# A tuned convolution and two feed-forward layers on one core: a new order of issue, the band in two halves, and other accumulators for block 1

## The chip, the cores and the metric

The program runs on one core of a Trainium2 chip. The core has a matmul engine (PE, with PEld its weight loads), a vector engine (DVE), an activation engine (ACT), a general engine (POOL) and a queue engine that issues most transfers (SP). Each works through its own list of instructions in order and waits on semaphores for the others. The metric is the device time of one execution in microseconds. The kernel before took a median of 1347.27 us over 3 runs (1347.11 to 1349.38).

## What is computed

Three stages follow each other on 8192 tokens (2 sequences of 4096) of 192 values. The first is a causal convolution of 7 taps, whose weights are a softmax per head; the two others are a product to 2048 hidden values, a function of each of them, and a product back to 192.

```python
out = np.einsum('hk,bskhg->bshg', softmax(weight), x_unf)       # 8 heads of 24 values
h = x @ w_in;   g = h * clip(h + 3, 0, 6) / 6;   x = g @ w_out     # layer 1
h = x @ w_in2                                                    # layer 2
P = a[0] + a[1]*h + a[2]*h**2 + a[3]*h**3
Q = 1.0 + abs(b[0])*abs(h) + abs(b[1])*h**2
out = (P / (Q + 1e-06)) @ w_out2
```

The weights of both layers come as 64-bit floats.

## The kernel before

The tokens are cut into 16 blocks of 512 columns, the last one into two units of 256. For each block the convolution is 8 matmuls per half (`conv`, L434, 4 heads each) with banded matrices that the program builds from the taps; ACT copies the result (L442), PE transposes it back (`flip`, L449), and ACT and DVE split it into a high and a low part (L464, L470, L473), since the large products run in a shortened float type, once per part.

A step is 128 of the hidden values. In layer 1, `mm1` (five matmuls, L493, from x1 tiles) fills a bank of PSUM; ACT (`u`, L537), DVE (`g`, L542), ACT (`hi1`, L549) and POOL (`lo1`, L555) make g in two parts, and `product_out` adds three matmuls of the high part (L510 to L512) and two of the low one (L507, L508) into two accumulators. In layer 2, `mm3` (five matmuls, L493, from x2 tiles) fills a bank, and the chain is longer: ACT `A` (L607), `t1` (L619) and in half of the steps `sq` (L626); POOL `S` (L628) or its product `q` (L640); DVE `t2` (L634) and `t3` (L646); ACT `R` (L651) and `RR` (L655, back into the bank); DVE `w` (L660), `p2` (L664, in the bank) and `G` (L669, reads the bank for the last time); ACT `hi2` (L675), POOL `lo2` (L684); then five matmuls into the accumulators again. Layer 1 fills banks 0 and 1 in turn, layer 2 banks 2 and 3, so `mm3` of a step can't start before `G` of the step two earlier. The last unit has more buffers and uses all four banks. Between the layers stand `x2ah`, `x2mh` and `x2mg` on ACT (L567 to L573) and `x2al`, `x2ml`, `x2mc` on DVE (L569 to L577); at a block's end of layer 2 come the copies `oa` and `oc` and the transposes to the output.

Eight tiles of weights per matrix are loaded by SP (`load_w`) and decoded from 64-bit words on ACT (L336), POOL or DVE (L341) and DVE (L359, L362, L366), during the first 120 us or so, while layer 1 of blocks 0 and 1 runs in turn, step by step.

Nothing of the order is left to a scheduler at compile time: every operation is entered with a due time in steps, an engine and a duration (`at`), and the class `Issue` plays a list schedule through (durations, and a `DELAY` from one engine to another), with some freedom to take a ready operation ahead of its due time (`AHEAD`, `LOOK`, the offsets `OFF`, the separate sets with 0 for the start and T for the end). The order so found is what each engine gets. Layer 1 takes 17 steps of that clock per block of 16 (`PER`), layer 2 takes 16.

In the start, a row of taps is written to DRAM (`line_d`) and read back as the band in one transfer (`load_band`, L277); five matmuls on a cleared tile (`warm`, L247) stand ahead of the convolution on PE. Convolution and transposes of blocks 0 and 1 share banks 0 and 1.

```python
    def transient(t, mm, ns, *args, r, kind):
        if t > end1:   # after the last of layer 1: its free accumulators
            tag = f"acc0{k % 2}"
        else:          # otherwise bank 0 or 1
            k = fill[0] % 2 if t < 0 else 0 if t < steps[0] else 1 - [k for w, k in line1 if w <= t][-1]
```

Of the kernel before, what the change touches and what calls it, by code (L numbers as in the profile page):

```python
# [19 lines left out]
CONV = -11  # L20
CONV2 = 0.8376
# [3 lines left out]
W1P = [-2.0905, -2.4299]  # L25
W2P = [2.9483, 2.117]
WARM = 5
LOENG = [0, 1, 0, 1]
CLAMP = [0, 1, 0, 1]
WPART = dict(c0=0.0562, v0=0.0087, vs=0.0665, h0=0.2619, hs=0.2434, l0=0.5102, ls=0.1416)  # L30
HEAD = 19.51
TAIL = -8.47
AHEAD0 = dict(P=25.956, A=43.027, V=18.922, G=37.877, S=999.0)
LOOK0 = dict(P=378, A=97, V=0, G=0, S=0)
AHEADT = dict(P=9.165, A=24.576, V=31.792, G=2.471, S=999.0)
LOOKT = dict(P=254, A=284, V=1155, G=896, S=0)
OFF0 = dict(
    mm2=-1.4892, mm2l=-1.3919, x2mh=-1.1097, x2mg=-0.0866, lo1=1.5742, x2ml=-0.9018, x2al=0.2383, x2mc=-0.3455,
    mm1=0.1136, hi1=0.7353, g=0.5771, u=0.4837, x2ah=-1.0749,
)  # L40
OFFT = dict(
    sq=0.1372, mm4l=-1.5612, x2al=2.84, RR=1.527, q2=0.2104, oa=0.7948, lo2=3.3259, mm3=-0.6693, q1=1.1422,
    A=-0.343, t3=0.9764, w=1.9701, G=2.497, x2mh=2.2752, x2mg=2.2815, x2ml=2.4515, hi2=2.9134, R=1.1819,
    p2=2.4131, tr=0.3535, q=-2.403, os=8.9369, mm4=-1.7015, x2mc=2.5635,
# [3 lines left out]
X0 = -3.2557  # L48
XW = [-105.8871, -99.8168, -59.3715, -39.2955]
BIAS = dict(l1=1.4587, dec=0.1797, conv=1.8628, out=-1.4432, x2=1.2507)  # L50
AHEAD = dict(P=17.791, A=45.084, V=20.941, G=8.591, S=999.0)
LOOK = dict(P=2, A=178, V=216, G=370, S=0)
OFF = dict(
    sq=-0.3729, q1=0.1602, q2=0.1324, mm3=-0.5533, mm1=0.6027, mm4=0.1407, tr=0.0986, mm2=0.6086, A=-0.3875,
    t1=0.044, u=0.6074, R=0.2641, RR=0.5103, hi2=1.3561, hi1=1.7136, S=-0.3298, lo2=1.7039, lo1=2.0429,
    q=-3.3751, t2=0.4308, t3=0.5046, w=0.5725, p2=0.7126, G=0.8821, g=1.0717, cv=0.9695, x1ah=0.9925,
    x1al=1.3455, x1bh=0.4453, x1bl=1.3457, x2ah=1.2164, x2al=2.2036, x2mh=1.1366, x2mg=2.4352, x2mc=2.0761,
    x2ml=1.54, oa=0.8735, oc=1.0231, os=1.0155, mm2l=0.8969, mm4l=0.5707,
# [3 lines left out]
class Issue:  # L62
# [4 lines left out]

    DELAY = dict(PP=0, PA=197, PV=197, AA=143, AV=148, AG=178, AP=270, VV=127, VA=128, VG=130, VP=256,  # L70
                 GG=80, GA=75, GV=130, GP=203, AS=100, VS=100, GS=100, SS=0)

    def __init__(self, rings, rule):
# [879 lines left out]
```

## Time and profile before

| | |
|---|---|
| median of 3 runs | 1347.27 us |
| the profiled execution | 1347.13 us, of which its span 1345.3 us and 1.83 us around it |
| busy share of the span | PE 96%, DVE 87%, ACT 89%, POOL 83% |
| granted TensorE clock, mean | 0.984 |
| first product of layer 1 / of layer 2 | at 28.37 / 122.74 us |

How to read it: the chain of work that ended last is 77% PE. Since matmuls overlap (a record lasts 0.39 us and the next starts 0.23 us after it), the busy share of PE says little of how densely it works; the distance from start to start does. The granted clock is a share of full speed: 1.00 is 2.4 GHz and 0.50 is 1.2 GHz. A wait names the instruction that came last.

### The profile page before, as it was taken

Reading aid. Unit: us, or ns where it says so; the run is one execution under the profiler, and the core shown is the slowest. Engines: PE = TensorE matmul, PEld = TensorE weight load, DVE = VectorE, ACT = ScalarE, POOL = GpSimd, SP = SyncE. Lnnn points to the kernel's source line nnn. Section 1 sums busy time; section 2 is a strip of 40 time slices with the busy share of each in tenths; the row PEclk is TensorE's granted clock in tenths of the full one; section 3 lists DMA queues with packets and bytes.
Section 4 is the critical chain, followed back from the end, with each engine's and each line's share of the span. In section 5 each row is a group of like instructions: output and inputs, shape, how many; then the busy total and the mean of one; then the engine's idle time right before and its main releaser. Section 6 shows DMA issues by size and latency. Waiting matters only on the chain.

```text
span 1345.3 us, 18628 instructions
## 1 busy us (share of the span) xinstructions
PE 1284.9 (96%) x6058; PEld 1049.4 (78%) x6058; DVE 1173.5 (87%) x1808; ACT 1195.6 (89%) x2183; POOL 1121.0 (83%) x954
## 2 busy tenths in 40 slices
PE   6999999999999999999999999999999999999986
PEld 4666887878878788787878878788877878887876
DVE  5988988888888888888888899888889888888887
ACT  4778999999989898999999989999999989988886
POOL 3987988888878888888888888888888888888875
PEclk7999999999999999999999999999999999999998
DMA  5441000000000000000000000000000000000000
GB/s 168 137 129 36 16 1 12 15 7 22 1 12 15 12 16 13 15 1 12 16 13 16 12 1 16 12 16 12 16 12 1 13 1 0 13 2 12 1 12 13
DMA packets 28986, 28.62 MB, mean 21 GB/s; under 512 B 2140, under 2 KB 25816, under 8 KB 28888
## 3 DMA queue, kind: packets, MB, share of 16 engines
q1 hardware_dynamic: 28728, 27.27, 6.7%
q8 instruction: 47, 0.77, 0.3%
q14 instruction: 51, 0.42, 0.1%
q10 hardware_dynamic: 160, 0.16, 0.0%
HBM read 21.13 MB, written 6.30 MB: 20 GB/s over the span
## 4 chain that ended last, share of the span: by engine, by line
PE 77%; ACT 10%; DVE 6%; POOL 3%; issue 2%; DMA 1%; POOLq 0%; DVEq 0%; ACTq 0%
PE bank L493 37%; PE acc L510 7%; PE acc L512 7%; PE acc L507 7%; PE acc L511 7%; PE acc L508 7%; PE bank L434 2%; ACT A L607 2%; POOL S L640 1%; PE bank L449 1%; ACT T L619 1%; ACT A L651 1%; POOL g2l L684 1%; ACT g2h L675 1%; ACT bank L655 1%
## 5 line engine op out<-in xcount | busy, mean ns | idle before, releaser
L640 POOL TENSOR_TENSOR S<-A,S 128x512 f32<-128x512 f32 x252 | 326.3, 1295 | 79.0 <-ACT S L626 65.6
L684 POOL TENSOR_TENSOR g2l<-T,g2h 128x512 fp32r<-128x512 f32 x252 | 326.5, 1296 | 38.7 <-ACT g2h L675 36.3
L555 POOL TENSOR_TENSOR g1l<-u,g1h 128x512 fp32r<-128x512 f32 x240 | 311.6, 1298 | 36.8 <-ACT g1h L549 31.7
L660 DVE SCALAR_TENSOR_TENSOR S<-S,bank 128x512 f32<-128x512 f32 x252 | 173.1, 687 | 95.0 <-ACT bank L655 92.1
L493 PE MATMUL bank<-low,B 128*128 128x512 f32 (+1 forms) x544 | 206.6, 380 | 0.2 <-DVE low L577 0.2
L634 DVE SCALAR_TENSOR_TENSOR T<-T,coef,bank 128x512 f32<-128x512 f32 x252 | 187.1, 742 | 11.2 <-ACT T L619 8.9
L646 DVE SCALAR_TENSOR_TENSOR T<-T,coef,bank 128x512 f32<-128x512 f32 x252 | 188.4, 747 | 8.2
L664 DVE SCALAR_TENSOR_TENSOR bank<-T,coef,bank 128x512 f32<-128x512 f32 x252 | 188.8, 749 | 0.0
L669 DVE SCALAR_TENSOR_TENSOR T<-S,bank 128x512 f32<-128x512 f32 x252 | 173.0, 687 | 8.5
L619 ACT ACTIVATE T<-bank,coef 128x512 f32<-128x512 f32 x252 | 173.5, 689 | 7.8 <-POOL g2l L684 5.0
L651 ACT ACTIVATE A<-S 128x512 f32<-128x512 f32 x252 | 159.8, 634 | 21.2 <-POOL S L640 19.3
L542 DVE SCALAR_TENSOR_TENSOR u<-u,bank 128x512 f32<-128x512 f32 x240 | 163.1, 681 | 14.3 <-ACT u L537 13.6
L675 ACT ACTIVATE g2h<-T 128x512 fp32r<-128x512 f32 x252 | 159.5, 633 | 8.2 <-DVE T L669 6.6
L655 ACT ACTIVATE bank<-A 128x512 f32<-128x512 f32 x256 | 154.1, 602 | 14.2 <-DVE T L646 9.9
L537 ACT ACTIVATE u<-bank 128x512 f32<-128x512 f32 x240 | 143.5, 599 | 17.2 <-PE bank L493 14.1
L549 ACT ACTIVATE g1h<-u 128x512 fp32r<-128x512 f32 x240 | 151.6, 636 | 2.6 <-DVE u L542 2.5
L493 PE MATMUL bank<-x2ah,Ah 128*128 128x512 f32 (+1 forms) x272 | 106.8, 393 | 22.7 <-DVE T L669 22.6
L628 POOL TENSOR_SCALAR S<-A,coef 128x512 f32<-128x512 f32 x126 | 97.2, 771 | 29.4 <-ACT A L607 28.4
L493 PEld LDWEIGHTS bank<-low,B 128*128 128x128 f32 x544 | 103.4, 190 | 19.8 <-DVE low L577 0.5
L510 PE MATMUL acc<-g2h,O 128*128 128x512 f32 (+1 forms) x280 | 110.9, 396 | 3.8 <-ACT g2h L675 3.5
L507 PE MATMUL acc<-g2l,O 128*128 128x512 f32 (+1 forms) x280 | 109.9, 394 | 4.5 <-POOL g2l L684 4.4
L493 PE MATMUL bank<-x1ah,Ah 128*128 128x512 f32 (+1 forms) x272 | 106.2, 390 | 5.5 <-DVE T L542 2.6
(126 smaller groups left out, 3232.1 us busy)
## 6 DMA issues: line engine op xcount, KB each, us to landing
raw<-in_moe_w_out_dram SPq DMA_DIRECT2D x16, 384.0 KB, 3.4
out_dram<-osb SPq DMA_DIRECT2D x32, 192.0 KB, 2.0
xn<-in_x_dram SPq DMA_DIRECT2D x14, 384.0 KB, 3.4
raw<-in_moe_w_in_dram SPq DMA_DIRECT2D x16, 256.0 KB, 2.9
raw<-in_moe_w_in_dram SPq DMA_DIRECT2D x16, 128.0 KB, 3.9
xn<-in_x_dram SPq DMA_DIRECT2D x16, 96.0 KB, 3.3
xn<-in_x_dram SPq DMA_DIRECT2D x2, 288.0 KB, 5.8
band<-line_d SPq DMA_DIRECT2D x1, 512.0 KB, 4.0
```

The lines of the kernel that those rows point to most:

```text
L493: nc.tensor.matmul(out=dst[:, cs], lhsT=w[nm][:, fs], rhs=m, start=(k == 0), stop=(k == 4))
L507: nc.tensor.matmul(out=a, lhsT=o[:, 0:128], rhs=g, start=False, stop=sp)
L510: nc.tensor.matmul(out=a, lhsT=o[:, 0:128], rhs=g, start=st, stop=False)
L555: nc.gpsimd.tensor_tensor(out=gl, in0=v1.pop((b, i)), in1=f32(g1[b, i][0]), op=ALU.subtract)
L619: act(out=v2[b, i]["T"], in_=h2[b, i], func=ACTF.Copy, scale=coef[:, 3:4])
L634: stt(out=d["T"], in0=d["T"], scalar=coef[:, 2:3], in1=h2[b, i], op0=ALU.add, op1=ALU.mult)
L640: (nc.gpsimd if k else nc.vector).tensor_tensor(out=d["S"], in0=d["A"], in1=d["S"], op=ALU.add if k == 1 else ALU.mult)
L646: stt(out=d["T"], in0=d["T"], scalar=coef[:, 1:2], in1=h2[b, i], op0=ALU.add, op1=ALU.mult)
L651: act(out=d["A"], in_=d["S"], func=ACTF.Abs_reciprocal_sqrt, bias=c1)
L660: stt(out=d["S"], in0=d["S"], scalar=c1, in1=h2[b, i], op0=ALU.add, op1=ALU.mult)
L664: stt(out=h2[b, i], in0=v2[b, i]["T"], scalar=coef[:, 0:1], in1=h2[b, i], op0=ALU.add, op1=ALU.mult)
L684: e.tensor_tensor(out=gl, in0=v2.pop((b, i))["T"], in1=f32(gh), op=ALU.subtract)
```

## The change

The tables that set the order are replaced, and the durations and delays from which it is planned. Two edits to the planner go with it: a reuse of a buffer by the same engine no longer asks for the end of the earlier use (`ops[p][2] != eng`), and durations of many operations come from a table by name (`NS`). The band is loaded in two transfers of 4 heads each, and each half of a convolution waits for its own. The convolution and transposes of block 1 go to the accumulators `acc10` and `acc11` (named `fb` in the profile), which layer 2 uses later, instead of banks 0 and 1. Twelve matmuls stand ahead of the convolution instead of five. Of the tables of numbers a line or two is shown.

```diff
-WARM = 5
+WARM = 12
-X0 = -3.2557
+X0 = -5.1761
+X1 = -0.8706
...
+    NS = dict(
+        mm1=1133, mm3=1133, conv=774, flip=445, out_tr=533, u=477, hi1=520, hi2=520, t1=568, R=520, RR=520,
...
     def at(self, t, eng, ns, f, *args, r=(), w=(), after=None, kind=None):
+        ns = self.NS.get(getattr(f, "__name__", ""), ns)
...
             for key in w:
-                pred.update((p, True) for p in read.pop(key, ()))
+                for p in read.pop(key, ()):
+                    pred[p] = pred.get(p, False) or ops[p][2] != eng
...
-    def load_band():
+    def load_band(half):
...
+        h = half * H // 2
+        nc.sync.dma_start(out=band[:, h:h + H // 2],
+                          in_=bass.AP(tensor=ld.tensor, offset=ld.offset + h * CW, ap=[[1, 128], [CW, H // 2], [1, 128]]))
...
-        if t > end1:
+        if t > end1 or mm in (conv, flip) and args[0] == 1:
             k = fill[0] = fill[0] + 1
-            tag = f"acc0{k % 2}"
+            tag = f"acc{int(t < end1)}{k % 2}"
...
-            at(t + D + OF["mm4"], "P", 648, product_out, 1, b, i, False, r=[Hi, ("Oh", 1, c), ("Ol", 1, c)], w=ac)
+            at(t + D + OF["mm4"], "P", 680, product_out, 1, b, i, False, r=[Hi, ("Oh", 1, c), ("Ol", 1, c)], w=ac)
...
-        t = when1(b, 0) + CONV if not first else X0 + b
+        t = when1(b, 0) + CONV if not first else X1 if b else X0
...
-            r = [("xn", b), ("band", 0)]
+            r = [("xn", b), ("band", hf)]
```

What stands on PE at the start of the program before: the matmuls of `warm`, both blocks' convolution (L434) and transposes (L449), then the first product of layer 1 (L493).

```order
L247 MATMUL warm<-idle 128x512 x5
L434 MATMUL bank_93<-xn,band 122x120 x4
L434 MATMUL bank_94<-xn,band 122x120 x4
L449 MATMUL bank_93<-perm,x1n 128x122 x5
L449 MATMUL bank_94<-perm,x1n 64x122 x5
L434 MATMUL bank_93<-xn,band 122x120 x4
L434 MATMUL bank_94<-xn,band 122x120 x4
L449 MATMUL bank_93<-perm,x1n 128x122 x5
L449 MATMUL bank_94<-perm,x1n 64x122 x5
L493 MATMUL bank_93<-x1ah,Ah_112 128x512
```

And in the changed kernel, where lines are 8 further down (L501 is the product of layer 1).

```order
L255 MATMUL warm<-idle 128x512 x12
L442 MATMUL bank_93<-xn,band 122x120 x4
L442 MATMUL bank_94<-xn,band 122x120 x4
L457 MATMUL bank_93<-perm,x1n 128x122 x5
L457 MATMUL bank_94<-perm,x1n 64x122 x5
L442 MATMUL fb<-xn,band 122x120 x8
L501 MATMUL bank_93<-x1ah,Ah_112 128x512
L501 MATMUL bank_93<-x1ah,Al_113 128x512
L501 MATMUL bank_93<-x1al,Ah_112 128x512
L501 MATMUL bank_93<-x1b,B_114 128x512
L501 MATMUL bank_93<-low_120,B_114 128x512
L457 MATMUL fb<-perm,x1n 128x122 x5
```

The first product of layer 1 for block 0 has moved ahead of the transposes of block 1, and block 1's work has left the banks.

The second place is PE at the end of a block of layer 1, in the middle of the program. Before, from the end of one `mm3` (bank_95) to the start of the next (bank_96):

```order
L493 MATMUL bank_95<-low_125,B_118 128x512
L510 MATMUL acc_5142<-g2h,O_119 128x512
L511 MATMUL acc_5142<-g2h,O_119 128x512
L512 MATMUL acc_5143<-g2h,O_119 128x512
L507 MATMUL acc_5142<-g2l,O_119 128x512
L508 MATMUL acc_5143<-g2l,O_119 128x512
L493 MATMUL bank_96<-x2ah,Ah_116 128x512
```

In the changed kernel, the last rows ahead of the same `mm3` (the 87th step of layer 2); the `mm3` before it stands 22 matmuls ahead.

```order
L515 MATMUL acc_5149<-g2l,O_119 128x512
L516 MATMUL acc_5150<-g2l,O_119 128x512
L518 MATMUL acc_5149<-g2h,O_119 128x512
L519 MATMUL acc_5149<-g2h,O_119 128x512
L520 MATMUL acc_5150<-g2h,O_119 128x512
L501 MATMUL bank_93<-x1ah,Ah_112 128x512
L501 MATMUL bank_93<-x1ah,Al_113 128x512
L501 MATMUL bank_93<-x1al,Ah_112 128x512
L501 MATMUL bank_93<-x1b,B_114 128x512
L501 MATMUL bank_93<-low_121,B_114 128x512
L501 MATMUL bank_96<-x2ah,Ah_116 128x512
```

What moved: before, five matmuls stand between two `mm3`; now products of layer 1 stand between them too. Over the 240 steps of layer 2 with 512 columns, the order before has 12 places, one per block of layer 1, with 5 to 7 matmuls there (and one pair at the start with none); the changed order has one such place, at the end.

## Rows read from the trace of the kernel before

**Rows 1.** Busy time by stage, all engines; the first line names the columns.

```profile
core 0: us, PE busy (x) PEld busy (x) DVE busy (x) ACT busy (x) POOL busy (x), PEclk, DMA share, GB/s
0.00:28.37 28.37, 18.52 (x62) 12.87 (x62) 15.16 (x42) 10.69 (x21) 9.96 (x18) 0.72 0.62 188
28.37:122.74 94.37, 87.23 (x362) 64.91 (x363) 84.01 (x170) 72.01 (x149) 75.86 (x74) 0.98 0.37 111
122.74:1233.39 1110.65, 1088.61 (x5072) 891.78 (x5071) 980.63 (x1456) 1023.23 (x1856) 953.01 (x794) 1.00 0.04 11
1233.39:1345.30 111.91, 90.55 (x564) 79.79 (x564) 93.66 (x142) 89.73 (x160) 82.18 (x70) 0.93 0.03 8
```

**Rows 2.** The same view, nine periods of layer 1 and one of them.

```profile
457.74:1191.29 733.55, 722.05 (x3334) 589.85 (x3334) 649.14 (x964) 678.41 (x1233) 633.37 (x528) 1.00 0.04 11
864.85:945.22 80.37, 79.92 (x369) 65.41 (x369) 72.11 (x108) 74.59 (x136) 68.94 (x58) 1.00 0.04 12
```

**Rows 3.** Timeline of PE: start us, us, engine, line, out<-in, count [idle before<-releaser].

```profile
533.25 0.27 PE L700 MATMUL bank<-perm,oac 128*128 128x128 f32 x1
...
533.79 0.47 PE L507 MATMUL acc<-g2l,O 128*128 128x512 f32 x1
...
543.68 0.39 PE L510 MATMUL acc<-g1h,O 128*128 128x512 f32 x1
...
545.72 0.39 PE L493 MATMUL bank<-low,B 128*128 128x512 f32 x1
...
560.79 1.86 PE L434 MATMUL bank<-xn,band 128*122 128x120 f32 x16
...
570.48 0.69 PE L449 MATMUL bank<-perm,x1n 122*128 122x122 f32 x5
```

**Rows 4.** Waits of PE, 122.74 to 1233.39 us: total us, times, longest.

```profile
PE bank L493 <- DVE T L669: 12.4, 14, 1.8
...
PE acc L510 <- ACT g2h L675: 2.3, 5, 0.6
```

**Rows 5.** Timeline of PE, two products into the same bank.

```profile
530.30 0.39 PE L493 MATMUL bank<-x2ah,Ah 128*128 128x512 f32 x1
...
538.76 0.50 PE L493 MATMUL bank<-x2ah,Ah 128*128 128x512 f32 x1 [0.48 <-DVE T L669]
```

**Rows 6.** Busy time by stretch, just after a wait of PE.

```profile
210.00:214.00 4.00, 3.56 (x9) 2.84 (x10) 3.79 (x6) 3.19 (x7) 3.55 (x5) 0.57 0.00 0
```

**Rows 7.** Waits of DVE, 122.74 to 1233.39 us.

```profile
DVE S L660 <- ACT bank L655: 85.7, 189, 1.4
```

**Rows 8.** Timeline of all engines, the start of the program.

```profile
1.30 6.64 PE L247 MATMUL warm<-idle 128*128 128x512 f32 x10 [1.30 <-POOL idle L905]
...
6.50 0.19 PEld L247 LDWEIGHTS warm<-idle 128*128 128x128 f32 x1 [0.24 <-issue]
...
6.93 0.19 PEld L247 LDWEIGHTS warm<-idle 128*128 128x128 f32 x1 [0.24 <-issue]
...
10.34 0.39 SPq L277 DMA_DIRECT2D band<-line_d  x1
...
14.39 3.63 PE L434 MATMUL bank<-xn,band 128*122 128x120 f32 x16 [6.44 <-DMA band<-line_d]
...
28.37 0.80 PE L493 MATMUL bank<-x1ah,Ah 128*128 128x512 f32 x1 [0.40 <-DVE x1al L470]
...
31.68 0.68 DVE L542 SCALAR_TENSOR_TENSOR u<-u,bank 128x512 f32<-128x512 f32 x1
```

**Rows 9.** Busy time by stretch, convolution of the first two blocks.

```profile
13.00:28.37 15.37, 11.87 (x52) 10.27 (x52) 7.00 (x15) 7.71 (x17) 3.71 (x4) 0.50 0.68 219
```

**Rows 10.** Groups of DVE, 28.37 to 122.74 us, shapes apart.

```profile
L366 DVE SCALAR_TENSOR_TENSOR m<-raw,bank 128x384 int32<-128x384 int32 x14 | 7.7, 547 | 0.0
```

**Rows 11.** Timeline of DVE, the last blocks.

```profile
1291.51 0.74 DVE L634 SCALAR_TENSOR_TENSOR T<-T,coef,bank 128x512 f32<-128x512 f32 x1
...
1295.83 0.74 DVE L634 SCALAR_TENSOR_TENSOR T<-T,coef,bank 128x512 f32<-128x512 f32 x1
```

More of the change, by code (lines that the diff above doesn't have):

```diff
@@ L20 @@
 CONV = -11
-CONV2 = 0.8376
+CONV2 = 1.4221
 PAT = [1, 2]
@@ L96, in graph @@
                         if len(line) >= ring:
-                            pred.update((p, True) for p in users[line[-ring]])
+                            for p in users[line[-ring]]:
+                                pred[p] = pred.get(p, False) or ops[p][2] != eng
                             gone.add(line[-ring])
@@ L106, in graph @@
             for key in w:
-                pred.update((p, True) for p in read.pop(key, ()))
+                for p in read.pop(key, ()):
+                    pred[p] = pred.get(p, False) or ops[p][2] != eng
                 written[key] = k
@@ L790, in conv_moe_moe_kernel @@
             at(t + OF["lo1"], "G", 1225, L1.lo1, b, i, r=[U, Hi], w=[Lo], kind="l1")
-            at(t + D + OF["mm2"], "P", 648, product_out, 0, b, i, False, r=[Hi, ("Oh", 0, c), ("Ol", 0, c)], w=ac, kind="l1")
-            at(t + D + OF["mm2l"], "P", 432, product_out, 0, b, i, True, r=[Lo, ("Oh", 0, c)], w=ac + [("sum", 0, b)] * (i == steps[b] - 1), kind="l1")
+            at(t + D + OF["mm2"], "P", 680, product_out, 0, b, i, False, r=[Hi, ("Oh", 0, c), ("Ol", 0, c)], w=ac, kind="l1")
+            at(t + D + OF["mm2l"], "P", 453, product_out, 0, b, i, True, r=[Lo, ("Oh", 0, c)], w=ac + [("sum", 0, b)] * (i == steps[b] - 1), kind="l1")
             t = when2(b, i)
@@ L823, in conv_moe_moe_kernel @@
             last = (b, i) == (NU - 1, steps[-1] - 1)
-            at(t + OF["lo2"], "V" if last else "G", 602 if last else 1225, L2.lo2, b, i, r=[T, Hi], w=[Lo])
-            at(t + D + OF["mm4"], "P", 648, product_out, 1, b, i, False, r=[Hi, ("Oh", 1, c), ("Ol", 1, c)], w=ac)
-            at(t + D + OF["mm4l"], "P", 432, product_out, 1, b, i, True, r=[Lo, ("Oh", 1, c)], w=ac + [("sum", 1, b)] * (i == steps[b] - 1))
+            at(t + OF["lo2"], "V" if last else "G", 605 if last else 1256, L2.lo2, b, i, r=[T, Hi], w=[Lo])
+            at(t + D + OF["mm4"], "P", 680, product_out, 1, b, i, False, r=[Hi, ("Oh", 1, c), ("Ol", 1, c)], w=ac)
+            at(t + D + OF["mm4l"], "P", 453, product_out, 1, b, i, True, r=[Lo, ("Oh", 1, c)], w=ac + [("sum", 1, b)] * (i == steps[b] - 1))
         t = when1(b, steps[b] - 1) + (D10 if b < 2 else D1)
@@ L854, in conv_moe_moe_kernel @@
         first = b < 2
-        t = when1(b, 0) + CONV if not first else X0 + b
+        t = when1(b, 0) + CONV if not first else X1 if b else X0
         if not b * C % S:
             at(-101 + b if first else t - 9, "V", 207, zero_x, b, w=[("xn", b)])
-        at(-100 + 45 * b if first else t - 8, "S", 1900, load_x, b, r=[("line_d", 0)] if b else [], w=[("xn", b)], after=1700)
+        at(-100 + 45 * b if first else t - 8, "S", 2400, load_x, b, r=[("line_d", 0)] if b else [], w=[("xn", b)], after=1700)
         where = {nm: OFF[nm] for nm in ("tr", "cv", "x1ah", "x1al", "x1bh", "x1bl")}
@@ L891, in conv_moe_moe_kernel @@
     for k in range(6):
-        at(-98 + k, "G", 600, zero_low, k, w=[("low", k)])
+        at(-98 + k, "G", 600, zero_low, k, r=[("line", 0)] if k else [], w=[("low", k)])
     for k, f in enumerate(band_ops()):
         at(-90 + k, "V", 75, f, r=[("tap", 0)], w=[("line", 0)])
-    at(-62, "S", 400, lambda: nc.sync.dma_start(out=line_d, in_=line), r=[("line", 0)], w=[("line_d", 0)], after=1700)
-    at(-60, "S", 1800, load_band, r=[("line_d", 0)], w=[("band", 0)], after=1700)
+    at(-62, "S", 400, lambda: nc.sync.dma_start(out=line_d, in_=line), r=[("line", 0)], w=[("line_d", 0)], after=2200)
+    for hf in range(2):
+        at(-60 + hf, "S", 1300, load_band, hf, r=[("line_d", 0)], w=[("band", hf)], after=1900)
     at(-99.4, "A", 400, lambda: nc.scalar.dma_start(out=perm, in_=ident), w=[("perm", 0)], after=3600)
@@ L906, in conv_moe_moe_kernel @@
     for k in range(WARM):
-        at(-104 + 0.01 * k, "P", 900, warm, r=[("idle", 0)], w=[("acc11", "warm")])
+        at(-104 + 0.01 * k, "P", 800, warm, r=[("idle", 0)], w=[("acc11", "warm")])
     with tc.manual_schedule():
```

59 lines of the change are left out of this document (29 added, 30 removed).

## The prediction

> **What bounds the kernel now.** I read the busy time by stage first [rows 1]. It splits the span into the convolution of the first two blocks (to 28.4 us), the stage in which weights are decoded while layer 1 of two blocks runs (to 122.7), the long middle in which layer 2 and layer 1 of a later block run together (1110.7 us, 83% of the span), and the last blocks (111.9 us). In the middle PE is busy for 98%, ACT for 92%, DVE for 88% and POOL for 86%: PE is next to its limit and the others are close behind it, so there is no large reserve. At the end PE is down to 81% and DVE stands at 84%.
>
> How near is PE to its limit in the middle? The nine periods from 457.74 to 1191.29 us take 733.55 us, 81.51 each [rows 2]; a period is 17 steps of layer 2 and 16 of layer 1, at ten matmuls each, so 330 matmuls. Nine starts in a row lie 2.04 us apart (543.68 to 545.72), 0.2267 each [rows 3], so 330 of them need 74.8. A convolution takes 1.86 at full clock, its two transposes 0.69 each, and half a block's output transposes 0.54 (533.25 to 533.79) [rows 3], with 2.125 halves per period 1.15. That makes 79.2; 2.3 us per period are lost. The middle has 1110.65 / 81.51 = 13.6 periods, so at most 31 us can be won there if the work itself stays.
>
> The Trainium skill ("Trainium Kernel Development and Optimization", Performance Expectations) calls matmul busy time a bad metric for the distance from the limit, because matmuls are pipelined. By busy time [rows 2] the room would be 11.5 us over nine periods, 17 us in the middle, and the gain taken below would use nearly all of it; by the distance of starts it is under half. The starts decide here, since a record lasts 0.39 us and the next follows after 0.23.
>
> Next the waits. In the middle PE waits 14 times, 12.4 us, for G of the step two earlier (DVE L669), and 2.3 us for g2h, of a total of 21.0 that the view names [rows 4]. One of them is at 538.76: the last `mm3` into this bank began at 530.30, 8.46 us earlier [rows 5]. That is how long a step of layer 2 holds its bank when nothing gives way. Two steps of PE take 2 x 81.51 / 17 = 9.6 us, so a step has about a microsecond to spare, and at the end of a block of layer 1, where the old order puts two `mm3` only 5 to 7 matmuls apart, the second comes too early.
>
> After two of these waits the clock falls: from 210 to 214 us, behind one of them, the granted clock is 0.57 [rows 6], between its levels of 2.4 and 1.2 GHz; 374 to 378 reads the same. PE loses 0.43 x 4 = 1.7 us in each.
>
> **The middle.** The tables of the plan and its durations move the whole order. The work is the same: as many matmuls and as many operations of each kind. What changes is seen in the order of PE: 11 of the 14 waits for G stand at one of the 12 places with 5 to 7 matmuls between two `mm3`; at the mean wait of 12.4 / 14 = 0.89 they are 9.7 us. The new order keeps only the twelfth place, behind the middle. I count the 9.7 as gone, the 2.3 for g2h with them (they follow right behind), and the 3.4 of clock: 15.4. What is late next is the copies: at a block's end ACT has six extra operations and DVE four, whoever waits for them, and ACT has only 8% free [rows 1]. So I keep a part back and take **-13**. A second sign points the same way: DVE waits 85.7 us for RR before `w` [rows 7], 0.38 us a step. On ACT's list 216 instructions stand between an R and its RR over 256 steps before, 155 now, so the chain through the bank gets shorter, not longer. Bounds: -31 if PE came to its 79.2 per period; above nothing, the third rival.
>
> **The start.** Before, conv of block 0 begins at 14.39, when the band lands, and the first product of layer 1 at 28.37 [rows 8], since it stands behind conv and transposes of block 1, which wait in turn until the banks have been read. The clock stands at half (0.50) all through [rows 9]; `warm` ended at 7.94, 6.4 us before the band. In the new order the first product waits only for block 0's chain and the eight matmuls of block 1's convolution. Block 0's chain took from 14.39 to 21.36 (when block 1's began, in the same steps: half of 28.37 - 14.39); with 3.63 for conv 1 the product would start at 25.0 at half clock. The twelve `warm` are 24 records: ten end at 7.94, and at 0.43 each (6.50 to 6.93) [rows 8] the other 14 end at 13.96, just ahead of the band, so PE is busy until it starts. At full clock a convolution takes 1.86 instead of 3.63, and the two transposes save 0.9 by the same ratio: 25.0 - 2 x 1.77 - 0.9 = 20.6, 7.8 us earlier than before. But DVE is what the next stage runs on (84.0 busy of 94.4 us [rows 1]), and it now reaches its first g (31.68 before [rows 8]) with less done: six decode operations of 0.55 us [rows 10] and block 1's two low parts of about 0.7 come after it, 4.7 us. Net 3.1; and as DVE isn't full in that stage I take **-4**, with 0 to -8 as bounds (half clock and all of it paid back; nothing paid back).
>
> The halves of the band I cost at nothing: the one transfer is issued at 10.34 and used at 14.39, the second half is issued 0.39 us later [rows 8] and so lands by 14.8 at worst, while the first half's four matmuls run. The cover is that half's 0.9 us; without it 0.4 is lost. SP's list has one issue more in the start, ahead of block 1's x, which is needed only after block 0's transposes. Accumulators `acc10` and `acc11` are wanted next by the first `product_out` of block 1, long after their transposes are read: nothing.
>
> The trace of before shows the clock low in that stretch. The Trainium skill ("TensorE: Matmul & The Clock Gate", What's actually happening) says that the low clock is the default, released by activity, and that the same kernel shows different numbers of slow matmuls from run to run. By that rule the seven extra `warm` can't be relied on: if the clock falls all the same, the start gives 0 and the sum is -15 instead of -19. One profile can't show it.
>
> **The last blocks.** In the order of DVE, 11 steps of layer 2 remain after the last x2 operation before, 14 now, so the last unit, with its four banks, can be mixed with the one before it three steps earlier. A step there took 4.32 us (1291.51 to 1295.83 [rows 11]) where DVE is busy for 84% [rows 1], 3.6: three steps at 0.7 are **-2**. Bounds -6 to +4, since the order of the very last steps is another one too, and the trace can't say what it costs.
>
> **Sum.** -13 - 4 - 2 = -19 against the profiled execution's 1347.13 us (span 1345.3 and 1.83 around it), which is the median of the runs to 0.14: **1328 us**, -1.4%.
>
> **The rivals.**
> 1. *The waits move.* ACT is at 92% and the copies at a block's end are still to be done; if PE waits as long as before, for x2 or g1h instead of G, the middle gives 0 to -4, and with -4 and -2 the time is 1337 to 1341. For it: ACT and DVE have little room. Against it: one period, from 864.85 to 945.22, takes 80.37 us [rows 2], so ACT and DVE can do 1.1 less than the mean.
> 2. *PE gets to its limit.* Most of the 2.3 us per period go, -24 in the middle, -7 in the start, -5 at the end: 1311. For it: fewer early `mm3` everywhere, not at the ends of blocks alone. Against it: no engine but PE could be late any more.
> 3. *Slower: the later second products hold the buffers.* From a step's `mm3` to the low part's product the new order has 64 matmuls in the mean, 57 before: 7 x 0.2267 = 1.5 us later, and g2h and g2l have two buffers each. If ACT's and POOL's writes two steps later wait for them, the delay goes on into R and G of the next steps. It decides from 19 / 240 = 0.08 us per step on; at 0.12 it is +29, the middle +16 and the time 1357. Against it: the longest distances were no shorter before (80 matmuls, 78 now).
>
> **How the numbers follow.** The forecast, with its own range of 1318 to 1338, has a chance of 0.6; rival 1 0.18, rival 2 0.12, rival 3 0.10. The range that is to hold 8 in 10 runs from 1312 (nearly all of rival 2 left below) to 1343 (rival 1 within, rival 3 outside). This kernel's runs can tell some 0.2%, 2.7 us, from no change. Faster than that are the forecast, rival 2 and nine tenths of rival 1 with a part of what lies between: 0.87; within it 0.05; slower 0.08 (rival 3 but for the cases in which it only eats the gain).
>
> **What would show it.** Right: the waits of PE for L677 (G) in the middle fall from 12.4 to under 3 us, a period of nine's mean to 80.5, no half clock between 200 and 400 us; the first product of layer 1 near 20.6 us at full clock and the first of layer 2 near 119; DVE's wait for RR shorter than 85.7. Wrong: as many waits of PE under another name (rival 1), POOL or ACT waiting for PE in the middle (rival 3), the clock at half through the convolution (the start), or a first product before 22 us with layer 2 still starting at 123, which would mean that DVE took all of it back.

## The result, and the profile after

The changed kernel takes a median of 1309.5 us (1309.26 to 1310.59, 4 runs) against 1347.19 in the same comparison (1345.51 to 1349.38, 4 runs): ratio 0.9721, 95% interval 0.9704 to 0.9738. The forecast of 1328 and its range from 1312 both lie above it. It is within 1.5 us of the time that rival 2 gave, 1311. One run of those below was slow, one of the ten of g1 at 4368.93 us: its ratio leaves it out, and its median would be 1345.74 without it.

The profiled execution has a span of 1308.8 us, 36.5 less. To see where they went, I cut both traces at the first product of layer 2 and at its 233rd (122.74 and 1233.39 us before). The busy times by stage, as in [rows 1], then nine periods as in [rows 2]:

```profile
core 0: us, PE busy (x) PEld busy (x) DVE busy (x) ACT busy (x) POOL busy (x), PEclk, DMA share, GB/s
0.00:20.59 20.59, 17.46 (x67) 9.83 (x67) 11.82 (x36) 7.26 (x14) 6.26 (x14) 1.00 0.65 183
20.59:112.67 92.08, 85.58 (x375) 64.68 (x373) 86.42 (x176) 73.86 (x156) 79.75 (x76) 1.00 0.44 131
112.67:1201.08 1088.41, 1085.29 (x5072) 887.19 (x5072) 973.73 (x1458) 1022.30 (x1856) 955.69 (x795) 1.00 0.04 11
1201.08:1308.80 107.72, 88.77 (x566) 78.10 (x564) 92.54 (x141) 88.67 (x160) 81.89 (x69) 0.94 0.03 8
438.55:1160.09 721.54, 721.09 (x3342) 589.39 (x3342) 644.62 (x964) 679.18 (x1231) 633.74 (x527) 1.00 0.04 11
```

Layer 2 starts 10.1 us earlier (122.74 - 112.67; forecast 4), the middle is 22.2 us shorter (1110.65 - 1088.41; forecast 13) and the end 4.2 (111.91 - 107.72; forecast 2). A period is 721.54 / 9 = 80.17 us instead of 81.51; the floor worked out for it was 79.2. The engines' busy times in the middle are nearly those of before: the work is the same, most of the gaps are gone.

All waits of PE that the view names in the middle (total us, times, longest), as in [rows 4]; they are 3.3 us, 21.0 before, and 1.1 of the 3.3, the wait for m, ends with the product at which the middle begins:

```profile
PE bank L501 <- DVE m L374: 1.1, 1, 1.1
PE bank L501 <- DVE T L677: 0.6, 1, 0.6
PE acc L518 <- ACT g1h L557: 0.5, 1, 0.5
PE acc L515 <- POOL g2l L692: 0.4, 1, 0.4
PE acc L515 <- POOL g1l L563: 0.4, 1, 0.4
PE bank L501 <- DVE Al L395: 0.3, 1, 0.3
```

By this view G (L677) was waited for 14 times, 12.4 us, and now once, 0.6. DVE's wait for RR, 85.7 before [rows 7]:

```profile
DVE S L668 <- ACT bank L663: 70.6, 143, 1.4
```

And PE at the start of the program (start, duration, line, operation, count), as in [rows 8]:

```profile
1.31 12.79 PE L255 MATMUL warm<-idle 128*128 128x512 f32 x24 [1.31 <-POOL idle L914]
15.26 1.94 PE L442 MATMUL bank<-xn,band 128*122 128x120 f32 x16 [1.17 <-DVE B L395]
17.86 1.26 PE L457 MATMUL bank<-perm,x1n 122*128 122x122 f32 x10 [0.66 <-ACT x1n L450]
18.96 1.87 PE L442 MATMUL fb<-xn,band 128*122 128x120 f32 x16
20.59 0.47 PE L501 MATMUL bank<-x1ah,Ah 128*128 128x512 f32 x1
```

Both convolutions run at full clock (1.94 and 1.87 us, 3.63 before), and the first product of layer 1 is at 20.59.

### The profile page after: what moved, and what is told of

Same layout as the page of the kernel before. It is cut to its first block, busy times and chain, and to the rows that moved or that the text cites. A ratio compares the mean times of both kernels' runs of the same rounds, so it can differ in the third digit from the quotient of the medians.

```text
span 1308.8 us, 18723 instructions
## 1 busy us (share of the span) xinstructions
PE 1277.1 (98%) x6072; PEld 1039.8 (79%) x6072; DVE 1164.5 (89%) x1808; ACT 1192.1 (91%) x2183; POOL 1123.6 (86%) x954
## 4 chain that ended last, share of the span: by engine, by line
PE 64%; DVE 16%; ACT 15%; issue 3%; POOL 2%; DMA 1%; SPq 0%; DVEq 0%; ACTq 0%; POOLq 0%
PE bank L501 30%; PE acc L518 6%; PE acc L515 6%; PE acc L520 6%; PE acc L519 6%; PE acc L516 6%; ACT bank L663 2%; DVE bank L672 2%; DVE S L668 2%; DVE T L654 2%; DVE T L677 2%; ACT A L659 2%; PE bank L442 2%; DVE T L642 2%; ACT A L615 2%
## 5 line engine op out<-in xcount | busy, mean ns | idle before, releaser
L501 PE MATMUL bank<-low,B 128*128 128x512 f32 (+1 forms) x544 | 205.4, 378 | 0.0
L550 DVE SCALAR_TENSOR_TENSOR u<-u,bank 128x512 f32<-128x512 f32 x240 | 163.1, 681 | 18.6 <-ACT u L545 18.1
L677 DVE SCALAR_TENSOR_TENSOR T<-S,bank 128x512 f32<-128x512 f32 x252 | 172.8, 686 | 7.2
L557 ACT ACTIVATE g1h<-u 128x512 fp32r<-128x512 f32 x240 | 151.4, 632 | 10.2 <-DVE u L550 9.9
L501 PE MATMUL bank<-x2ah,Ah 128*128 128x512 f32 (+1 forms) x272 | 110.3, 406 | 12.5 <-DVE T L677 9.9
L501 PEld LDWEIGHTS bank<-low,B 128*128 128x128 f32 x544 | 102.4, 188 | 19.6
L501 PE MATMUL bank<-x1ah,Ah 128*128 128x512 f32 (+1 forms) x272 | 105.1, 386 | 3.2 <-DVE u L550 2.9
```

The costliest lines, as they stand in the source:

```text
L501: nc.tensor.matmul(out=dst[:, cs], lhsT=w[nm][:, fs], rhs=m, start=(k == 0), stop=(k == 4))
L677: stt(out=d["T"], in0=d["S"], scalar=2.0, in1=h2.pop((b, i)), op0=ALU.subtract, op1=ALU.mult)
```

## The experiments

The traces leave two questions. In the middle: did the waits go because the places without layer-1 products went (theory 1), because of the new offsets (theory 2), or because the copies on ACT and DVE moved (theory 3)? In the start: is the earlier first product paid back by DVE (theory B) or kept (theory A)? All runs in one table. "Layer 2", "middle" and "end" are differences to the profiled execution of before, cut at the same two products; the ratio is to runs of before on the same chip. A column compares one execution with one, and before alone ran from 1341.3 to 1351.6 us beside g1 to g4, so a microsecond or two in it says little.

| run | median us | ratio (95% interval) | layer 2 | middle | end |
|---|---|---|---|---|---|
| after | 1309.5 | 0.9721 (0.9704-0.9738) | -10.1 | -22.2 | -4.2 |
| e1 start edits alone | 1340.4 | 0.9956 (0.9941-0.9971) | -7.9 | -1.1 | +0.4 |
| e2 durations alone | 1322.1 | 0.9819 (0.9805-0.9834) | -0.9 | -23.7 | -1.7 |
| e3 PE's durations alone | 1326.2 | 0.9850 (0.9834-0.9866) | -1.2 | -16.5 | -2.8 |
| e4 all but PE's | 1338.3 | 0.9944 (0.9927-0.9960) | -4.2 | -3.3 | -0.5 |
| f1 durations and start | 1315.2 | 0.9766 (0.9752-0.9781) | -9.4 | -22.1 | -1.1 |
| f2 after without start edits | 1311.6 | 0.9740 (0.9726-0.9755) | -8.0 | -23.0 | -5.4 |
| f3 after, 5 warm | 1311.6 | 0.9742 (0.9727-0.9757) | -8.0 | -22.3 | -5.0 |
| f4 before, copies later | 1351.9 | 1.0040 (1.0025-1.0055) | +1.6 | +5.9 | -1.7 |
| g1 PE at 104.6% | 1345.8 | 0.9998 (0.9983-1.0013) | -4.9 | +2.8 | -1.8 |
| g2 after, old durations | 1346.8 | 1.0008 (0.9992-1.0024) | -13.6 | +14.3 | -1.8 |
| g3 after, PE at 95.4% | 1323.7 | 0.9844 (0.9825-0.9862) | -12.0 | -9.4 | -3.9 |
| g4 after, old end tables | 1317.3 | 0.9801 (0.9783-0.9819) | -10.7 | -22.1 | +3.9 |
| h1 PE at 97.8% | 1328.4 | 0.9867 (0.9839-0.9895) | -1.6 | -16.4 | -0.6 |
| h2 PE at 98.9% | 1326.1 | 0.9851 (0.9822-0.9880) | -1.4 | -19.0 | -0.6 |
| h3 PE at 101.1% | 1324.6 | 0.9843 (0.9813-0.9874) | -4.8 | -16.5 | -1.8 |
| h4 PE at 102.2% | 1325.8 | 0.9844 (0.9815-0.9873) | -4.1 | -15.1 | -2.0 |
| i1 PE at 95.4%, rest as e3 | 1343.1 | 0.9988 (0.9973-1.0004) | -2.3 | -1.7 | -1.2 |
| i2 after, PE at 101.1% | 1322.9 | 0.9832 (0.9809-0.9854) | -9.2 | -12.1 | -2.2 |

**e1, the start edits alone.** WARM, X0 and X1, the halves of the band and the accumulators of block 1, on the kernel before.

```diff
-WARM = 5
+WARM = 12
...
-        if t > end1:
+        if t > end1 or mm in (conv, flip) and args[0] == 1:
...
-    at(-60, "S", 1800, load_band, r=[("line_d", 0)], w=[("band", 0)], after=1700)
+    for hf in range(2):
+        at(-60 + hf, "S", 1300, load_band, hf, r=[("line_d", 0)], w=[("band", hf)], after=1900)
...
```

> The kernel before with the start edits alone: 12 matmuls of warm-up, the band matrices in two halves, block 1's convolution and flips in layer 2's accumulators, and X0 and X1 of the kernel after; every duration and every other table as before. Theory A (the lead is kept: the first layer-1 product comes 7.8 us earlier and DVE makes good the work that this puts off, because its idle time in the dense stage shrinks): the first product of layer 2 starts 8 to 12 us earlier than 122.74, the middle and the end stay as they were, 1335 to 1340 us. Theory B, the prediction's step (4.7 us of DVE work put off is paid back later): 3 to 5 us earlier, 1342 to 1345 us. If the middle's order also changes through the earlier start, the period of a block moves from 81.5 us; neither theory expects that.

Two rows of the PE timeline, and the busy times from one to the other:

```profile
20.65 0.50 PE L481 MATMUL bank<-x1ah,Ah 128*128 128x512 f32 x1
...
114.87 0.39 PE L481 MATMUL bank<-x2ah,Ah 128*128 128x512 f32 x1
```

```profile
20.65:114.87 94.22, 86.88 (x373) 64.44 (x372) 86.11 (x176) 73.02 (x155) 79.23 (x77) 1.00 0.40 122
```

The first product of layer 1 is 7.7 us earlier than before (28.37), the first of layer 2 7.9 (theory A said 8 to 12): nothing is paid back. DVE does 2.1 us more in this stretch (86.1 against 84.0 [rows 1]) in the same length: it takes the deferred work out of its idle time. Theory A holds. The median is 5.6 us under before's 1346.07, just outside theory A's range, though the profiled execution, the fastest of its four at 1338.8, lies in it and has 8.6 us less span; by the ratio's interval the gain is 4 to 8 us.

**e2, the durations alone.** The table of durations, `DELAY` and the reuse rule on the kernel before. 1133 ns is five times the 0.2267 us from start to start of [rows 3]; before planned 1083.

```diff
+    NS = dict(mm1=1133, mm3=1133, conv=774, flip=445, out_tr=533, u=477, hi1=520, hi2=520,
...
...
-            at(t + D + OF["mm4"], "P", 648, product_out, 1, b, i, False, ...
+            at(t + D + OF["mm4"], "P", 680, product_out, 1, b, i, False, ...
...
```

> The kernel before with the planner's measured durations and delays alone (and the rule that a buffer's reuse on the same engine costs no delay): its start, its offsets and look-aheads as before. The order then has 2 places with fewer than 9 matmuls between two first products of layer 2, where before had 13. Theory 1 (the places at which TensorE has no layer-1 product left beside the chain are what the middle paid for, and the durations alone remove them): middle 15 to 22 us shorter, PE's waits for G there under 4 us, 1322 to 1332 us. Theory 2 (the gain is in the newly tuned offsets): places or not, the middle keeps its 81.5 us a block, 1343 to 1350 us.

PE's waits in the middle, all that the view names:

```profile
PE bank L500 <- DVE T L676: 2.0, 4, 1.0
PE acc L517 <- ACT g1h L556: 1.7, 1, 1.7
```

The time is in theory 1's range and far from theory 2's: the whole gain of the middle (23.7 us, where 15 to 22 were expected) comes without one new offset.

**e3 and e4, the durations divided.** e3 has only those of PE's operations, e4 all the others.

```diff
+    NS = dict(mm1=1133, mm3=1133, conv=774, flip=445, out_tr=533)          # e3
...
+    NS = dict(u=477, hi1=520, hi2=520, t1=568, R=520, RR=520, ...          # e4
...
```

> The kernel before with only TensorE's durations changed in the planner (first products 1133 in place of 1083 ns, second ones 680 and 453 in place of 648 and 432, convolution 774, flips 445, output transposes 533). Its order has 4 places with fewer than 9 matmuls between two first products of layer 2, none of them at the ends of blocks. Theory 1a (the planner thought TensorE 4.6% faster than it is, so its plan ran out of layer-1 products at the end of each block): most of what the full set of durations gives, 1322 to 1335 us. Theory 1b (the durations of ACT and DVE matter as much): less than half of it, 1338 to 1347 us.

> The kernel before with every new duration, delay and the reuse rule except TensorE's. The order keeps 14 places with fewer than 9 matmuls between two first products of layer 2. Theory 1a (TensorE's durations decide): the waits for G stay, 1341 to 1350 us. Theory 1b (the other engines' durations decide): 1322 to 1335 us, with the waits for G gone although the places stand.

e3's and e4's waits of PE for G in the middle, first e3:

```profile
PE bank L496 <- DVE T L672: 2.3, 5, 0.9
```

```profile
PE bank L500 <- DVE T L676: 13.3, 12, 1.9
```

Theory 1a: PE's durations give 16.5 of the 23.7 us, the others alone 3.3. The two don't add up (19.8); I read it that the rest is worth something only once PE is planned right. In e4 the places stand, and so do the waits, though its median, 1338.3, lies between the ranges of the two theories.

**f1 and f2, do the parts add?** f1 is e1 and e2 together, with before's offsets; f2 is the kernel after without its start edits.

```diff
-WARM = 12                                                               # f2, against after
+WARM = 5
...
-            tag = f"acc{int(t < end1)}{k % 2}"
+            tag = f"acc0{k % 2}"
...
```

> The kernel before with the measured durations and delays and the start edits together, and every offset and look-ahead as before. If the two gains are separate, they add: the run with the start edits alone had its first product of layer 2 7.9 us earlier, that with the durations alone a middle 23.7 us shorter and an end 1.7 us shorter, so 1347 - 33 = 1314 us, 1311 to 1318. If the earlier start is paid back in a middle that now has no slack (DVE's deferred work, the prediction's step), the middle is 3 to 5 us longer than with the durations alone: 1317 to 1321 us.

> The kernel after with the start of before: 5 matmuls of warm-up, one band matrix, block 1's convolution in the banks, X0 of before. Its durations and offset tables are those of the kernel after. If the offset tables give nothing beyond the durations: as with the durations alone, 1320 to 1325 us. If they give the part of the start and the end that the durations and the start edits leave open (2.2 us at the start, 2.5 us at the end): 1316 to 1320 us.

f1 adds: 1315.2, in the predicted 1311 to 1318. f2 does better than either expectation. Its first product of layer 1 comes 5.5 us later than in after, yet layer 2 starts only 2.1 later:

```profile
26.05 0.51 PE L488 MATMUL bank<-x1ah,Ah 128*128 128x512 f32 x1 [0.89 <-DVE x1al L465]
...
114.77 0.48 PE L488 MATMUL bank<-x2ah,Ah 128*128 128x512 f32 x1 [1.09 <-DVE m L361]
```

```profile
26.05:114.77 88.72, 83.15 (x361) 64.11 (x362) 84.12 (x171) 71.39 (x150) 78.15 (x75) 1.00 0.40 122
```

DVE is idle for 4.6 of 88.7 us here, and the last decode on it (L361) is what the first product of layer 2 waits for; in after it is the same line (m L374, 1.1 us, above). So after's durations and offsets without the start edits (f2), and the start edits alone (e1), each bring layer 2 forward by some 8 us, and all together by 10. In the traces of before, after, e1, e2, f1, f2 and f3 DVE has been busy for 98 to 100 us when layer 2 starts (before 15.16 + 84.01, after 11.82 + 86.42); what differs is its idle time, 23.6 us before and 14.4 after.

**f3, the warm-up.** After's order word for word, with 5 of its 12 matmuls.

```diff
+        if f is warm:
+            seen += 1
+            if seen > 5:
+                continue
...
```

> The kernel after in its own order word for word, but only 5 of the 12 matmuls of the warm-up are issued. TensorE is then idle from about 8 us to the first convolution, and the granted clock falls to half as in the kernel before. Theory A (what the first product loses, the end loses): the first layer-1 product 3 to 5 us later than 20.59, the first product of layer 2 as much later, 1312 to 1315 us. Theory B, the prediction's step turned round (the stage before layer 2 is bound by DVE's work, which the clock of TensorE doesn't change): the first product of layer 2 less than 1.5 us later, 1309 to 1311 us. If the warm-up's length has nothing to do with the clock, the first product stays at 20.6 us and the time at 1309.5.

The first products of the two layers:

```profile
23.04 0.48 PE L501 MATMUL bank<-x1ah,Ah 128*128 128x512 f32 x1
...
114.75 0.47 PE L501 MATMUL bank<-x2ah,Ah 128*128 128x512 f32 x1 [1.11 <-DVE m L374]
```

2.45 us later at layer 1, 2.08 at layer 2. What the start loses there is kept lost, as theory A says, but it is less than the 3 to 5 us expected. Part of that is where the convolution began: at 14.26 here, and at 15.26 in after's profiled execution, which issued the band 0.93 us later (11.29 against 10.36). From the start of the convolution to the first product f3 takes 8.78 us and after 5.33, so the lower clock costs 3.45. By time f3 can't be told from after (intervals 0.9727-0.9757 and 0.9704-0.9738), and its median lies between the ranges of both theories. The clock part is clear over all runs: from 14.6 to 19.0 us the granted clock is 1.00 in all 7 profiles with 12 matmuls, and 0.50 to 0.65 in all 13 with 5.

**f4, the copies.** The kernel before in its own order, with copies at a block's end set behind the next RR (ACT) or G (DVE). A copy moves only where that RR or G is among the next four operations of its engine and nothing that needs the copy comes first; by the order in the two traces 18 of 68 moved on ACT and 18 of 68 on DVE.

```diff
+        past = {"A": L2.RR, "V": L2.G}
+        for c in [e for e in seq if e[1] in (x2_op, out_ev) and 2 <= e[2][0] < NB - 1]:
...
+                seq.insert(to, seq.pop(i))
...
```

> The kernel before in its own order, but each copy at a block's end (outputs to their tile on ACT, the next block's operands on DVE) stands behind the next RR (ACT) or G (DVE) instead of ahead of it. TensorE's order is unchanged, with its 12 places of too few layer-1 products. Theory 1 (those places make the wait): PE's waits for G stay at 9 us or more in the middle, 1342 to 1351 us. Theory 3 (the copies between R and RR, and before G, make the chain late): the waits for G fall under 4 us, 1330 to 1339 us.

```profile
PE acc L510 <- ACT g2h L675: 8.0, 11, 1.2
PE bank L493 <- DVE T L669: 7.4, 11, 1.5
```

The kernel is slower (1.0040), against theory 3. The wait for G does fall, from 12.4 to 7.4, under the 9 that theory 1 expected: the copies that moved had a part in it. But a wait for g2h takes its place, 8.0 instead of 2.3. The two together stood at 14.7 before [rows 4] and stand at 15.4 here, so no time was to be won from the place of these copies; the others were not moved.

**g1, too long instead of too short.** e3 with PE's products 4.6% above what they take.

```diff
-    NS = dict(mm1=1133, mm3=1133, conv=774, flip=445, out_tr=533)
+    NS = dict(mm1=1185, mm3=1185, conv=774, flip=445, out_tr=533)
...
```

> The kernel before with TensorE's products planned 4.6% longer than they take (first products 1185 ns, second ones 711 and 474) in place of 4.6% shorter; nothing else differs from the run with TensorE's measured durations (1326.2 us). Theory 1c (it is enough that the plan does not take TensorE for faster than it is; too long a duration only leaves the plan slack): 1322 to 1330 us. Theory 1d (a duration off to either side empties or crowds TensorE at the block ends alike): half of the gain is lost, 1334 to 1342 us.

```profile
117.87:1231.37 1113.50, 1100.45 (x5072) 883.82 (x5071) 980.61 (x1458) 1025.23 (x1858) 954.02 (x795) 1.00 0.04 11
```

The whole gain is gone, more than theory 1d said, though the order has only one place with fewer than 9 matmuls. The view names 5.3 us of waits for G, and PE's busy time is 12 us above before's. But the view counts idle time, and a record of PE lasts longer than the distance to the next start, so a short wait can hide in it. One of many places, three rows of PE and one of DVE:

```profile
341.43 0.39 PE L511 MATMUL acc<-g2l,O 128*128 128x512 f32 x1
341.95 0.50 PE L496 MATMUL bank<-x2ah,Ah 128*128 128x512 f32 x1
342.29 0.40 PE L496 MATMUL bank<-x2ah,Al 128*128 128x512 f32 x1
```

```profile
341.21 0.69 DVE L672 SCALAR_TENSOR_TENSOR T<-S,bank 128x512 f32<-128x512 f32 x1
```

G ends at 341.90. The `mm3` starts 0.05 us later, 0.52 behind the product ahead of it instead of 0.23, and no idle time is shown. I counted the `mm3` of the middle that start 0.25 us or more behind the last product and within 0.06 us of the end of a G: 47 in g1, which lose 12.7 us, 7 in e3 (3.4), 20 in e2 (5.1), 15 in before (15.3) and 23 in after (3.6). Each is followed by the next product 0.34 us later instead of 0.23, which adds 5.2 us in g1 and 0.8 in e3. Of the 19.3 us between the middles of g1 and e3 some 14 (9.3 and 4.4) are the wait for G again, in many short pieces. Theory 1 as I had it, that it suffices to remove the places, falls here: G can come late without them.

**g2 and g3, after with wrong durations.** g2 has all of before's, g3 only those of PE's products.

```diff
-        mm1=1133, mm3=1133, conv=774, ...                               # g3, against after
+        mm1=1083, mm3=1083, conv=774, ...
...
```

> The kernel after with the durations, delays and reuse rule of before: its offsets, look-aheads and start edits stay. The order has 6 places with fewer than 9 matmuls between two first products of layer 2, 4 of them in the middle's first 70 steps. If durations and offsets only work together: the start keeps 8 to 10 us, the middle gains less than half, 1322 to 1333 us. If the offsets are what the middle gained by: 1308 to 1316 us. If the middle is as before: 1335 to 1339 us.

> The kernel after with TensorE's products planned at the old, too short durations (1083, 648, 432 ns), all else as in after. With after's offsets the order still has only 2 places with fewer than 9 matmuls between two first products of layer 2. If the order that comes out is what counts (the places), the numbers being only a way to it: 1307 to 1314 us. If a plan with TensorE too fast lets the other engines run late whatever the places: the middle loses as between the runs with and without TensorE's durations, 1320 to 1330 us.

After's offsets with before's durations are worth nothing (1.0008), which is slower than any of the three expectations: layer 2 starts 13.6 us earlier and the middle gives back 14.3. PE's waits for G there:

```profile
PE bank L494 <- DVE T L670: 11.4, 16, 2.1
```

g3 loses 14.2 us against after, 12.8 of them in the middle, at 2 places as in after (one of them the pair at the start). PE's waits for G are 7.2 us there, 11 times. Again the count of places doesn't tell the time.

**g4, the end.** After with before's OFFT, AHEADT and LOOKT.

```diff
-AHEADT = dict(P=10.587, A=26.994, V=26.868, G=6.693, S=999.0)
+AHEADT = dict(P=9.165, A=24.576, V=31.792, G=2.471, S=999.0)
-LOOKT = dict(P=716, A=250, V=265, G=983, S=0)
+LOOKT = dict(P=254, A=284, V=1155, G=896, S=0)
...
```

> The kernel after with before's three tables for the last blocks (offsets, look-aheads in time and in places). If these tables gave the end its 4.2 us: the stretch from the 233rd first product of layer 2 to the end is 2.5 to 4 us longer, 1311.5 to 1314 us. If the end gained by the measured durations: within 1 us of after, 1308.5 to 1310.5 us.

The end is 8.1 us longer than in after, twice what was expected, and 3.9 longer than before's own. The two largest waits of PE from 1200.62 us on:

```profile
PE bank L488 <- DVE T L664: 11.0, 8, 2.7
PE acc L505 <- ACT g2h L670: 4.6, 4, 2.2
```

The end's tables are fitted to what precedes them; they are worth 8 us on after's order. On before's, with the durations alone, the end gained 1.7 without them.

**h1 to h4 and i1, a row over PE's durations.** e3 with the products at 97.8, 98.9, 101.1 and 102.2% of the measured value; i1 is at before's 95.4%, and so parts the products from convolution, flips and output transposes, which e3 also corrects.

```diff
-    NS = dict(mm1=1133, mm3=1133, conv=774, flip=445, out_tr=533)
+    NS = dict(mm1=1108, mm3=1108, conv=774, flip=445, out_tr=533)          # h1
...
```

> The kernel before with TensorE's products planned at 97.8% of the measured durations (1108, 665, 443 ns). Theory P (the places decide; the order has none at block ends but one): as with the measured durations, 1324 to 1329 us. Theory D (the durations must be right, the loss graded between 1326 at 100% and 1346 at 95.4%): 1332 to 1340 us. Theory L (each order is good or bad by chance): no relation to its neighbours.

> As before it, at 98.9% (1121, 673, 448 ns). Theory P: 1324 to 1329 us. Theory D: 1328 to 1334 us. Theory L: no relation to its neighbours.

> At 101.1% of the measured durations (1145, 687, 458 ns). Theory P: 1324 to 1329 us. Theory D, with the loss graded up to 1346 us at 104.6%: 1328 to 1334 us. Theory L: no relation to its neighbours.

> At 102.2% of the measured durations (1158, 695, 463 ns). Theory P: 1324 to 1329 us. Theory D: 1332 to 1340 us. Theory L: no relation to its neighbours.

> The kernel before with only the measured durations of convolution, flips and output transposes (774, 445, 533 ns); the products keep 1083, 648 and 432 ns. The order has 14 places with fewer than 9 matmuls between two first products of layer 2, at every block end. If the products' durations, and the places that they make, are the cause: waits for G of 9 us or more in the middle, 1341 to 1351 us. If the three small kinds are: 1324 to 1330 us.

In order of the duration the medians are 1343.1 (95.4%, i1), 1328.4, 1326.1, 1326.2 (100%), 1324.6, 1325.8 and 1345.8 (104.6%). Five neighbours agree to 4 us, so this is not chance (theory L), and there is no least at 100% (theory D): it is a flat stretch with a step to either side. On the flat stretch, and from it down to 95.4%, theory P fits: the order has 14 places with fewer than 9 matmuls at 95.4%, and 3 or 4 at the five, one of them at a block's end where before had one too; g1 shows that above it the places don't decide. PE's waits for G at 95.4% (i1) and 97.8% (h1):

```profile
PE bank L496 <- DVE T L672: 12.8, 13, 1.9
```

```profile
PE bank L496 <- DVE T L672: 3.8, 7, 1.6
```

**i2, after at 101.1%.**

```diff
-        mm1=1133, mm3=1133, ...
+        mm1=1145, mm3=1145, ...
...
```

> The kernel after with TensorE's products planned 1.1% longer (1145, 687, 458 ns). If after's offsets stand on the flat stretch that the runs on before showed between 97.8 and 102.2%: 1306 to 1313 us. If they fit their durations to a per cent: 1314 to 1322 us.

After's offsets fit their durations to a per cent: 13.4 us are lost by a change that on before's offsets does nothing (e3 to h3). The view names no more waits for G than in after, and the middle is 10.2 us longer all the same (the 2.7 for m end where it begins):

```profile
PE bank L501 <- DVE m L374: 2.7, 1, 2.7
PE bank L501 <- DVE T L677: 0.6, 3, 0.2
```

```profile
113.58:1212.16 1098.58, 1093.73 (x5077) 887.71 (x5078) 974.60 (x1458) 1022.82 (x1855) 955.94 (x797) 1.00 0.04 11
```

Its PE is busy for 1093.7 us, 8.4 more than in after. Here too the starts tell more: 40 `mm3` start late right behind a G, 6.6 us against 3.6 in after, the products that follow them add 4.4 against 2.5, output transposes start late behind `g` of layer 1 (L550) 10 times, 3.0 us against 0.5, and one stretch of low clock, which after doesn't have, costs 1.7. That is 9.1 of the 10.2. So in g1 and i2 most of the loss is known by name. Why a plan with too long a duration lets G come late, no run isolates; that stays open.

## Why the prediction was wrong

*The middle, -13 against -22.2.* The mechanism was the one named, waits of PE and for G above all, with the clock behind them. What was counted came, and more: G fell from 12.4 to 0.6 by the view (11.8, where 9.7 were counted), g2h from 2.3 to nothing, and the 3.4 of clock came whole, since the clock was low in two stretches before [rows 6] and in none of the middle after. The step that failed is the next one, "What is late next is the copies", with "ACT has only 8% free" and "So I keep a part back". It took 2.4 us off, and it put at nothing the other waits in the total of 21.0, though it names the total. Before, these were:

```profile
PE acc L510 <- ACT g1h L549: 3.0, 5, 1.8
...
PE acc L507 <- POOL g2l L684: 2.1, 3, 0.9
PE acc L510 <- DVE x2al L569: 1.0, 2, 0.5
PE bank L493 <- DVE low L577: 0.2, 1, 0.2
```

They fell from 6.3 to 0.9 us. With G, g2h and the clock that is 22.9, less 0.7 for two small waits that only after has (its 1.1 for m lies ahead of the middle), so 22.2 where 22.2 were measured. That it fits so closely is partly chance, since waits that are hidden in records are not in it (G in after: 3.6 by the starts, 0.6 by the view). No copy is late: the view of PE's waits names none, and f4 won nothing by moving some. A share of 92% busy in ACT was no sign that ACT would be the bound: its work stayed the same, and it is busy for 94% now. The argument against rival 2 ("no engine but PE could be late any more") describes nearly what happened; with -22.2, -10.1 and -4.2 for its -24, -7 and -5 it deserved more than 0.12. What the prediction didn't see is that the places are only one way to such waits: in g1 they come without them.

*Where it came from.* The prediction put the durations and the tables in one term. e2 and g2 part them: the durations give the whole of the middle, the offsets without them nothing. The change's 37.7 us are some 24 of durations, 7 more by the start edits (f1) and 5.7 by the offsets on top of both (1315.2 to 1309.5), of which the traces show 3.1 in the end, 0.7 at the start of layer 2 and next to nothing in the middle. In the other order the offsets give 10.5 (e2 to f2) and the start edits 2.1. The offsets' part comes only at exactly these durations (i2, g3).

*The start, -4 against -10.1.* The first product was forecast at 20.6 and came at 20.59, at full clock. The clock was reasoned rightly, and it was full in all seven profiles with twelve matmuls of warm-up; that the time fits so well is luck. The convolution began at 15.26, not at 14.39, since the band was issued later (11.29 against 10.34), and from there to the product it took 5.33 us where the working has 6.2. g4, with the same start, has 14.50 and 19.75. The Trainium skill ("TensorE: Matmul & The Clock Gate", What's actually happening) has the number of slow matmuls vary from run to run; by that the lead could have been lost, and no run here shows it. The step that failed is "4.7 us after it. Net 3.1". The deferred work was real (2.4 us more on DVE in the dense stage), but I made it a debt to be paid in time, where DVE had 10.4 us idle in that stage to do it in: e1 kept the whole lead. Of the 2.2 us between e1's 7.9 and the 10.1, 1.5 come with the durations (f1 has 9.4 with before's offsets) and 0.7 with the offsets; the prediction gave neither anything there. f2 reaches 8.0 without the start edits, by the same reserve of idle time, so the parts don't add. The halves of the band were not quite free: e1 waits 0.40 us for the second, which it uses from 15.98 on, where the forecast had it landed by 14.8 at worst.

*The end, -2 against -4.2.* The term "three steps at 0.7 are -2" was mis-sized, and its reason was incomplete: g4 shows that the tables for the end are worth 8 us on this order. PE still waits for G there (10.2 us before, 9.3 after); the end has no layer 1 to fill in.

*DVE's wait for RR* fell to 70.6 as forecast (below 85.7), the period to 80.17 (80.5 forecast), and neither rival 1 nor rival 3 came.

## What to carry to other kernels

Plan an order with durations taken from start to start on the engine that bounds the program, and try them some per cent to either side: here, with before's offsets, 2% made no difference and 4.6% cost everything, and with after's 1.1% cost 13 us. When waits go away on the bounding engine, and the others do the same work as before, count all waits the view names, not those with the nicest explanation, and don't hold gain back only because another engine is at 90%. Where records overlap, read the starts too: a view of idle time can leave out most of a wait (12.7 us against 5.3 in g1). Work that is moved behind another step costs only what the idle time there can't take; so compare it with that idle time, and offsets that were tuned with one set of durations should not be carried to another.

## What was not expected of the hardware

Stretches of low clock in the middle cost alike: summed over 4 us windows, 1.72 us are lost in e2 and in e3, which have one, and 3.44 in before and e1, which have two. g3 has one that costs twice as much. Each begins during a wait of PE or within some 2 us behind one. The row of e2, behind a wait of 1.71 us that ends at 129.39:

```profile
129.80:133.80 4.00, 3.81 (x11) 2.72 (x10) 3.76 (x6) 2.78 (x6) 2.19 (x2) 0.63 0.00 0
```

But the length of the wait doesn't decide. h3 has a low stretch behind 1.33 us, and before waits 1.78 us ahead of the product at 457.74, e4 1.90 at 1102.66 and g1 2.40 at 124.96, without any. e3 and h2 wait equally long for the same g1h, and the clock falls in e3 alone (0.57 from 130 to 134 us, 1.00 in h2):

```profile
128.49 0.50 PE L513 MATMUL acc<-g1h,O 128*128 128x512 f32 x1 [1.80 <-ACT g1h L552]
```

```profile
128.32 0.50 PE L513 MATMUL acc<-g1h,O 128*128 128x512 f32 x1 [1.80 <-ACT g1h L552]
```

What decides it, these runs don't tell.

A product that had to wait also delays the next one: behind each of the 47 late `mm3` of g1 the next product starts 0.33 to 0.34 us later, where the usual distance is 0.23.
